# Three more zero fills write 56 KB rows in a decode-attention training kernel on one Trainium2 core

## The chip, the cores and the metric

The kernel runs on one core of one Trainium2 (trn2) chip. The metric is device time in microseconds (us) of one execution. Timed runs of the same kernel agree within about 0.1% here (765.08 to 765.98 us over all timed runs of the kernel before; the execution that was profiled took 766.4 us), so differences below about 1 us in the time need several rounds, and below 0.3 us they can't be seen at all. Engines are named as in the profile: PE multiplies matrices, DVE and ACT work on vectors, POOL issues the zero fills, SP and ACT also issue the other transfers.

Three sources are used. The *page* and the *views* of the profile (groups, waits, timeline, windows) are shown as they stand. The trace behind them also has one record for each DMA packet (here one row of a transfer, or one completion, which is a write of 4 bytes), with queue, start, duration and size; what is read from these is said to come from the packet records, and is of one execution for each kernel.

## The reference, cut to what matters

One decode step of attention with a gated MLP, and the gradients of all inputs. The caches are 32768 positions long, but only the last 4096 positions of each head take part:

```python
B, Sq, D = 2, 1, 512
Hq, Hkv, Sk, Dh = 32, 8, 32768, 128
W = min(4096, max(256, Sk // 4))            # 4096
k = jnp.repeat(k_cache[:, :, Sk - W:, :], rep, axis=1)
v = jnp.repeat(v_cache[:, :, Sk - W:, :], rep, axis=1)
...
_out, _vjp = jax.vjp(_f, A_x, A_k_cache, A_v_cache, A_wq, A_wo, ...)
```

The gradients of the two caches are therefore zero at 28672 of 32768 positions of each of 2 x 16 heads. The output must have these zeros, and writing them is most of what the kernel does: 32 regions of 28672 x 128 bf16 numbers, 7.34 MB each, 235 MB of 327 MB that are moved in all.

## The kernel before: the parts that matter

Zeros come from one tile `zt` in on-chip memory (SBUF) of 128 partitions x 14336 bytes. A fill is a DMA issued from POOL that converts while it copies: the 14336 bytes become 14336 bf16 numbers (28672 B) or, where the output is viewed as 4-byte numbers, 57344 B.

```python
ZR = SK - W                  # 28672 positions
ZG = 112
zt = const.tile([P, ZG * DH], mybir.dt.uint8, name="zt")
...
def zf(o, q, r0, nent, rows, rep=1):         # nent rows of `rows` positions, rep times
    b, hk = divmod(q, HKV)
    nr = nent * rows * rep
    v = o[b, hk, r0:r0 + nr, :]
    w = rows * DH
    if w > ZG * DH:                          # a row of 224 positions: 57344 B
        v = v.bitcast(F32)
        w //= 2
    v = v.rearrange("(r p g) d -> p r (g d)", p=nent, g=rows)
    st = 4 if nent < 16 else 1
    zs = zt[0:nent * st:st, 0:w].unsqueeze(1).to_broadcast([nent, rep, w])
    sw_fill.append(nc.gpsimd.dma_start(out=v, in_=zs))
    return r0 + nr
...
zlong = (0, 1, 3, 5, 7, 11, 12, 16, 17, 18, 19, 22, 23, ...)
zshort = {2: ((5, 8, 2), (120, 68, 3), ...), 4: ..., 20: ...}   # eight fills, divided
...
for qi in range(ZQ - 1):                     # ZQ = 32: 31 fills on POOL's software queue
    r = 0
    whole = (P, ZR // P, 1) if qi in zlong else (P, ZG, ZR // (P * ZG))
    for n, rows, rep in zshort.get(qi, (whole,)):
        r = zf(*zparts[qi], r, n, rows, rep)
```

So an undivided fill in `zlong` is 128 rows of 57344 B; the three that are not (9, 14, 21) are 256 rows of 28672 B. Eight more are cut into pieces, not changed here. The 32nd fill is issued by SP at the very end, in rows of 14336 B.

Beside the fills run four rounds, each of four heads: a 4 MB V load and a 4 MB K load (SP), computation, and two 4 MB stores of gradients (ACT), each load waiting for the store that frees its buffer. Then come the weight gradients and the last fill:

```python
last = nc.sync.dma_start(out=out_6.rearrange("(p k) f -> p k f", k=DK), in_=dw1_st)   # dW1
...
with tc.issue_after(last.ins):
    fin = nc.sync.dma_start(out=v, in_=zs)   # the 32nd fill, after dW1 in SP's order
tc.add_manual_dep(fin.ins, sw_fill[-2].ins.name, ...)   # and after the last but one on POOL
```

Of the kernel before, what the change touches and what calls it, by code (L numbers as in the profile page):

```python
# [16 lines left out]
def kernel(  # L17
# [86 lines left out]
    ZQ = 2 * B * HKV  # L104
    zparts = [(out_2, q) for q in range(B * HKV)] + [(out_3, q) for q in range(B * HKV)]

    zlong = (0, 1, 3, 5, 7, 11, 12, 16, 17, 18, 19, 22, 23, 24, 25, 26, 27, 28, 29, 30)
    zshort = {
        2: ((5, 8, 2), (120, 68, 3), (128, 32, 1), (16, 1, 1)),
        4: ((3, 1, 2), (2, 99, 6), (128, 112, 1), (128, 102, 1), (86, 1, 1)),  # L110
# [564 lines left out]
```

## Time and profile before

| | before |
|---|---|
| time, median (runs) | 765.66 us (3) |
| span of the profiled run | 764.6 us |
| moved | 326.73 MB |
| PE / DVE / ACT busy | 51% / 36% / 28% |
| dW1 store issued (end of computation) | 696.9 us |
| final fill issued, landed | 724.2, 763.4 us |

The page of the kernel before, its parts 1 to 3. The DMA row gives the mean busy share of the 16 DMA engines in 40 equal slices of the span, in tenths; the queue lines give packets, MB, and the share of 16 engines' span:

```profile
span 764.6 us, 9391 instructions
...
PE 388.6 (51%) x4109; PEld 234.4 (31%) x4118; DVE 275.8 (36%) x483; ACT 214.9 (28%) x313; POOL 34.7 (5%) x67
...
DMA  9999999999999999999999999999999999999998
...
DMA packets 12217, 326.73 MB, mean 427 GB/s; under 512 B 2898, under 2 KB 2906, under 8 KB 2934
...
q0 software_dynamic: 7744, 227.55, 70.3%
q1 hardware_dynamic: 2696, 56.63, 20.8%
q10 hardware_dynamic: 1736, 41.95, 13.9%
```

No engine is near its limit except the DMA engines, which never have a free slice. Queue q0 holds the fills of POOL, q1 what SP issues, q10 what ACT issues.

The windows view of the kernel before, three stretches: columns are the stretch, its length, busy time of PE, PEld (PE's weight loads), DVE, ACT and POOL, the clock granted to PE, DMA share, GB/s:

```profile
528.00:556.00 28.00, 16.27 (x272) 12.61 (x270) 13.54 (x26) 10.52 (x10) 1.59 (x3) 0.84 1.03 436
560.00:600.00 40.00, 26.07 (x253) 14.76 (x256) 13.97 (x30) 11.95 (x20) 1.04 (x2) 0.76 1.02 432
725.00:740.00 15.00, 0.00 (x0) 0.00 (x0) 0.00 (x0) 0.00 (x0) 0.00 (x0) 0.50 1.06 434
```

The rate is the same with computation (first two lines) and without (third line): transport doesn't wait for computation. A window counts a packet with the stretch in which it starts, so a short one can read some GB/s too high or too low; counted by overlap, stretches of 20 us from 40 to 760 us carry 429 to 433.

The timeline of SP's DMA issues in the kernel before (start, duration, line of the kernel, what), the last loads and the end:

```profile
479.04 0.54 SPq L210 DMA_DIRECT2D nat<-in_A_v_cache_dram  x1
501.42 0.54 SPq L210 DMA_DIRECT2D nat<-in_A_k_cache_dram  x1
...
696.91 0.33 SPq L639 DMA_DIRECT2D out_dram<-dw  x1
724.24 0.39 SPq L644 DMA_DIRECT2D out_dram<-zt  x1
```

And four lines of its waits views, the last from that of SP's queue (who waited for whom, us in total, times, longest):

```profile
POOL out_dram L101 <- DMA out_dram<-zt: 507.8, 39, 27.3
...
PE tp L387 <- DMA nat<-in_A_v_cache_dram: 126.5, 3, 52.2
...
PE tp L387 <- DMA nat<-in_A_k_cache_dram: 11.3, 2, 9.5
...
SPq L644 <- DMA out_dram<-zt: 26.9, 1, 26.9
```

After the dW1 store at 696.9 us nothing is left but transfers. The final fill then stands behind another fill for 27 us. POOL's issuing is no limit either: it waits 508 us for earlier fills to land.

### The profile page before, as it was taken

Reading aid. Unit: us, or ns where it says so; the run is one execution under the profiler, and the core shown is the slowest. Engines: PE = TensorE matmul, PEld = TensorE weight load, DVE = VectorE, ACT = ScalarE, POOL = GpSimd, SP = SyncE. Lnnn points to the kernel's source line nnn. Section 1 sums busy time; section 2 is a strip of 40 time slices with the busy share of each in tenths; the row PEclk is TensorE's granted clock in tenths of the full one; section 3 lists DMA queues with packets and bytes.
Section 4 is the critical chain, followed back from the end, with each engine's and each line's share of the span. In section 5 each row is a group of like instructions: output and inputs, shape, how many; then the busy total and the mean of one; then the engine's idle time right before and its main releaser. Section 6 shows DMA issues by size and latency. Waiting matters only on the chain.

```text
span 764.6 us, 9391 instructions
## 1 busy us (share of the span) xinstructions
PE 388.6 (51%) x4109; PEld 234.4 (31%) x4118; DVE 275.8 (36%) x483; ACT 214.9 (28%) x313; POOL 34.7 (5%) x67
## 2 busy tenths in 40 slices
PE   0566774477007747830784770038459467594000
PEld 0543553333005534410463320026344333321000
DVE  3234342485003446430554650014344245663000
ACT  0044521455001246530224550002422254153000
POOL 0200100010000000000000000000000000000000
PEclk9986997778556867665596775559859666555555
DMA  9999999999999999999999999999999999999998
GB/s 378 434 410 428 447 420 425 442 438 414 437 423 435 429 435 431 426 433 425 430 430 445 430 422 438 422 436 424 440 442 430 430 425 432 432 427 428 442 409 367
DMA packets 12217, 326.73 MB, mean 427 GB/s; under 512 B 2898, under 2 KB 2906, under 8 KB 2934
## 3 DMA queue, kind: packets, MB, share of 16 engines
q0 software_dynamic: 7744, 227.55, 70.3%
q1 hardware_dynamic: 2696, 56.63, 20.8%
q10 hardware_dynamic: 1736, 41.95, 13.9%
q8 instruction: 32, 0.52, 0.3%
q14 instruction: 9, 0.07, 0.0%
HBM read 45.62 MB, written 280.50 MB: 427 GB/s over the span
## 4 chain that ended last, share of the span: by engine, by line
DMA 32%; PE 31%; DVE 13%; ACT 9%; issue 6%; ACTq 0%; SPq 0%; DVEq 0%
DMA out_dram<-nat 14%; DMA nat<-in_A_v_cache_dram 8%; DMA nat<-in_A_k_cache_dram 7%; PE tp L387 6%; PE ov L421 5%; ACT tring L150 3%; DMA b_bf<-in_B_b_dram 2%; ACT p_bf L455 2%; ACT nat L150 2%; DVE tring L152 2%; PE s_ps L394 2%; DVE nat L152 2%; DVE ds_bf L468 2%; PE wps L588 2%; PE dops L314 2%
## 5 line engine op out<-in xcount | busy, mean ns | idle before, releaser
L387 PE MATMUL tp<-pperm,nat 128*128 128x128 bf16 x1024 | 91.9, 243 | 144.7 <-DMA nat<-in_A_v_cache_dram 126.5
L152 DVE COPY tring<-tp 128x1024 bf16<-128x1024 bf16 (+1 forms) x98 | 65.9, 689 | 179.1 <-PE tp L387 169.4
L387 PEld LDWEIGHTS <-nat 128*128 128x128 bf16 x1024 | 68.5, 109 | 165.1 <-DMA nat<-in_A_v_cache_dram 128.4
L150 ACT CAST nat<-ov 128x512 bf16<-128x512 f32 x160 | 87.7, 589 | 68.8 <-PE ov L421 48.1
L150 ACT COPY tring<-tp 128x1024 bf16<-128x1024 bf16 (+1 forms) x34 | 34.4, 1011 | 228.5 <-PE tp L387 155.1
L152 DVE CAST nat<-ov 128x512 bf16<-128x512 f32 x96 | 65.6, 690 | 59.7 <-PE ov L421 57.1
L101 POOL DMA_DIRECT2D out_dram<-zt x58 | 33.1, 576 | 529.3 <-DMA out_dram<-zt 507.8
L421 PE MATMUL ov<-bd,ds_bf 128*128 128x512 bf16 x124 | 49.4, 472 | 6.6 <-DVE nat L152 3.9
L421 PE MATMUL ov<-bd,p_bf 128*128 128x512 bf16 x123 | 47.3, 451 | 5.5 <-DVE nat L152 1.4
L410 PE MATMUL ps<-t,nat 128*128 128x16 bf16 x1024 | 28.7, 173 | 14.3 <-DVE bd L375 7.2
L410 PEld LDWEIGHTS <-nat 128*128 128x128 bf16 x1024 | 28.7, 103 | 17.1 <-issue 11.9
L394 PEld LDWEIGHTS <-zz 128*32 128x32 bf16 x512 | 17.8, 96 | 33.4 <-issue 23.1
L152 DVE CAST wq<-wps 128x512 bf16<-128x512 f32 x16 | 11.0, 690 | 42.4 <-PE wps L581 42.3
L402 PE MATMUL tp<-ident_bf,p_bf 128*128 128x128 bf16 x64 | 7.6, 312 | 34.9 <-ACT p_bf L455 34.9
L394 PE MATMUL s_ps<-tring,zz 128*32 128x256 bf16 x256 | 19.2, 288 | 11.8 <-ACT tring L150 7.4
L394 PE MATMUL dp_ps<-tring,zz 128*32 128x256 bf16 x256 | 20.5, 326 | 7.1 <-ACT tring L150 4.2
L150 ACT CAST wq<-wps 128x512 bf16<-128x512 f32 x16 | 9.4, 586 | 51.7 <-PE wps L581 51.7
L455 ACT ACTIVATE p_bf<-e_sb,rl 32x512 bf16<-32x512 f32 x16 | 22.8, 1424 | 3.4 <-DVE rl L452 3.2
L468 DVE SCALAR_TENSOR_TENSOR ds_bf<-dp_ps,delta,p_bf 32x512 bf16<-32x512 f32 x16 | 21.7, 1355 | 0.2
L421 PEld LDWEIGHTS <-ds_bf 128*128 128x128 bf16 x128 | 13.1, 110 | 20.6 <-issue 18.3
L421 PEld LDWEIGHTS <-p_bf 128*128 128x128 bf16 x128 | 12.9, 110 | 19.6 <-issue 16.7
L564 PE MATMUL tp<-ident_bf,wq 128*128 128x128 bf16 x128 | 16.8, 248 | 2.3 <-issue 2.3
(195 smaller groups left out, 435.5 us busy)
## 6 DMA issues: line engine op xcount, KB each, us to landing
out_dram<-zt POOLq DMA_DIRECT2D x23, 7168.0 KB, 100.0
out_dram<-nat ACTq DMA_DIRECT2D x8, 4096.0 KB, 40.5
out_dram<-zt POOLq DMA_DIRECT2D x7, 3584.0 KB, 71.3
nat<-in_A_v_cache_dram SPq DMA_DIRECT2D x4, 4096.0 KB, 31.8
nat<-in_A_k_cache_dram SPq DMA_DIRECT2D x4, 4096.0 KB, 26.6
out_dram<-zt SPq DMA_DIRECT2D x1, 7168.0 KB, 39.5
out_dram<-zt POOLq DMA_DIRECT2D x2, 3488.0 KB, 66.9
out_dram<-zt POOLq DMA_DIRECT2D x1, 6120.0 KB, 67.6
```

The source lines that it names most:

```text
L101: sw_fill.append(nc.gpsimd.dma_start(out=v, in_=zs))
L150: nc.scalar.copy(out=out_ap, in_=in_ap)
L152: nc.vector.tensor_copy(out=out_ap, in_=in_ap)
L314: nc.tensor.matmul(dops[0:B, :, :], lhsT=dsT_bf[:, dk, :], rhs=woT[:, :, dk, :], start=(dk == 0), stop=(dk == DK - 1))
L387: nc.tensor.transpose(tp[:, j, :], nat[:, g * CC + half * CH + j, :], pperm[:].rearrange("p b k -> p (b k)"))
L394: nc.tensor.matmul(out_ps[pr * RB:(pr + 1) * RB, half * CH * PB:(half + 1) * CH * PB], lhsT=zbuf[:, pr, o:o + RB], rhs=tT[:, :, pr, :], st ...
L410: nc.tensor.matmul(ps[:], lhsT=nat[:, g * CC + half * CH + cc, :], rhs=cols[half][:, cc, :, g, :], start=(half == 0 and g == 0 and cc == 0 ...
L421: nc.tensor.matmul(ov[:], lhsT=src[:, cc].rearrange("r k b -> r (k b)"), rhs=bd[:, gh * 4:(gh + 1) * 4, :], start=True, stop=True)
L455: nc.scalar.activation(out=p_bf[rb, :, :, pr], in_=e_sb[rb], func=ACT.Copy, scale=rl[rb, 0:1])
L468: nc.vector.scalar_tensor_tensor(out=ds_bf[rb, :, :, pr], in0=dp_c[rb], scalar=delta[rb, 0:1], in1=p_bf[rb, :, :, pr], op0=ALU.subtract, o ...
L564: nc.tensor.transpose(tp[:, jj, :], wq[:, k, n0:n0 + DH], ident_bf[:, :])
L588: nc.tensor.matmul(wps[:], lhsT=o_rows[:, j:N:NJ], rhs=ds_rows[:, :], start=True, stop=True)
```

## The change

The intent is that every undivided fill writes the longer rows: half as many packets for the same bytes.

```diff
-    zlong = (0, 1, 3, 5, 7, 11, 12, 16, 17, 18, 19, 22, 23, 24, 25, 26, 27, 28, 29, 30)
+    zlong = (0, 1, 3, 5, 7, 9, 11, 12, 14, 16, 17, 18, 19, 21, 22, 23, 24, 25, 26, 27, 28, 29, 30)
```

## The prediction

> **What bounds the kernel now.** Transport. The page's DMA row is 9 in 39 of 40 slices; 326.73 MB in 764.6 us are 427 GB/s. In the trace's packet records an engine stands idle for less than 0.1 us (mean of 16) in every 20 us from 20 to 760 us; only the first 5 us and the last 1.9 us are thin (the engines finish between 761.5 and 763.4 us). PE is busy 51%, DVE 36%, ACT 28%. The timeline shows the last computation at about 697 us; after it only transfers run, and the last zero fill (7168 KB, issued by SP at 724.2 us after a wait for another fill) lands at 763.4. So the end is set by bytes over rate. The Trainium skill agrees ("DMA: Bandwidth & Descriptors", Specifications: a fabric ceiling of 435 GB/s); the windows 560:600 and 725:740 show 432 and 434.
>
> **What the change does.** Fills 9, 14 and 21 (7.34 MB each) go from 256 rows of 28672 B to 128 rows of 57344 B. Bytes, DMA count (58 on POOL), dependencies and engines stay; 384 packets leave the software queue (7744 to 7360). In the packet records a 28672 B packet takes 1079 ns median (1082 mean), a 57344 B one 2155 (2150 mean). Two short ones cost 3 to 14 ns more than one long one. 384 pairs over 16 engines: 0.07 to 0.34 us saved. Pool's issue (0.55 us median) hides behind waits for other fills (508 us over 39 waits), so anything saved there is worth nothing.
>
> **What moves.** Packets alternate between queues one by one: at 700:716 us the fills, SP and ACT share 236, 62 and 135 GB/s, the ratio of their rows (57, 14, 33 KB). The skill states that round-robin ("Queues, rings and completion order", Arbitration). So longer fill rows take a larger share from the loads beside them. Fill 9 now runs at about 240 to 267 us beside the second K load, fill 14 at about 357 to 393 beside the third K load, fill 21 at about 490 to 540 beside the last V and K loads. An even split of 32 KB and 28 KB rows gives a load 53%, beside 56 KB rows 36%: 18 us against 27 us for 4 MB. I expect these loads to land 3 to 9 us later, and the computation to end 5 to 15 us later (702 to 712 us). That is off what sets the end: the fills get what the loads lose, a fill of 17 us lies behind the software queue's end, and the engines stay full as long as the last stores are issued before about 740 us.
>
> **Predicted.** 765.3 us, 0.3 below; 8 in 10 between 764.3 and 766.7, mostly for the 1 to 2 us with which the engines finish unequally, which another order of packets can shift. Chances: faster 0.01, same 0.98, slower 0.01.
>
> **What would show it.** Packets in the software queue 7360, no 28672 B packets except in the divided fills; rate beside those fills up by under 1%; the K and V loads named land later; the last computation after 697 us; the final fill still ends about 763 us; DMA row unchanged.
>
> **What would make it wrong.** If the longer rows delay the last stores past 740 us, the tail runs dry and the loss is real. If one DMA engine is slower than the others and gets relief from fewer rows, the end could move by a microsecond or two. If computation has less slack than I read, it would be slower by several us.

## More of the kernel before

A packet record doesn't say on which of the 16 DMA engines it ran.

## The result, and the profile after

| | before | after |
|---|---|---|
| time, median of 6 runs each | 765.51 us | 765.31 us |
| lowest to highest | 765.24 to 765.92 | 765.06 to 765.58 |
| packets in the software queue | 7744 | 7360 |
| second K load complete | 254.4 us | 261.0 us |
| third K load complete | 388.3 us | 397.9 us |
| last V load complete | 507.0 us | 511.7 us |
| last K load complete, 15th and 16th completion | 525.2, 525.8 us | 528.2, 555.6 us |
| dW1 store issued | 696.9 us | 724.6 us |
| last packet of POOL's fills / of all | 745.8 / 763.4 us | 727.2 / 762.1 us |

The ratio is 0.9996, with a 95% interval of 0.9984 to 1.0009: the same. The completions and the last packets come from the packet records: each load posts 16 four-byte completion packets, and the load has landed when the sixteenth has ended.

The page after, the lines that answer to those of before:

```profile
span 763.3 us, 9400 instructions
...
PE 387.6 (51%) x4118; PEld 233.5 (31%) x4118; DVE 275.8 (36%) x483; ACT 214.6 (28%) x313; POOL 34.0 (4%) x67
...
DMA  9999999999999999999999999999999999999998
...
DMA packets 11833, 326.73 MB, mean 428 GB/s; under 512 B 2898, under 2 KB 2906, under 8 KB 2934
...
q0 software_dynamic: 7360, 227.55, 70.5%
```

384 packets fewer, the same bytes, the same rate, the same rows of nines. The windows after:

```profile
528.00:556.00 28.00, 1.52 (x23) 0.85 (x20) 1.04 (x2) 1.01 (x1) 1.06 (x2) 0.58 1.06 434
560.00:600.00 40.00, 20.50 (x331) 15.64 (x330) 17.47 (x29) 12.60 (x13) 0.53 (x1) 0.67 1.02 432
725.00:740.00 15.00, 0.00 (x0) 0.00 (x0) 0.00 (x0) 0.00 (x0) 0.00 (x0) 0.50 1.03 440
```

The first line is the surprise. Between 528 and 556 us PE now works 1.5 us, where it had worked 16.3, while the DMA engines move as much as ever. SP's timeline and the waits after say why and where it goes:

```profile
482.61 0.54 SPq L210 DMA_DIRECT2D nat<-in_A_v_cache_dram  x1
507.46 0.54 SPq L210 DMA_DIRECT2D nat<-in_A_k_cache_dram  x1
...
724.57 0.33 SPq L639 DMA_DIRECT2D out_dram<-dw  x1
725.00 0.42 SPq L644 DMA_DIRECT2D out_dram<-zt  x1
```

```profile
POOL out_dram L101 <- DMA out_dram<-zt: 507.8, 38, 28.4
...
PE tp L387 <- DMA nat<-in_A_v_cache_dram: 130.0, 3, 49.7
...
PE tp L387 <- DMA nat<-in_A_k_cache_dram: 42.8, 4, 25.3
```

PE waits 31.5 us longer for K loads, and one wait, for the last of them, is 25.3 us long. Computation ends 27.7 us later, and none of that reaches the time, which is as before. But the 27 us between the dW1 store and the final fill are used up: the final fill is now issued 0.4 us after that store, so it is SP's order and no longer another fill that holds it.

### The profile page after: what moved, and what is told of

Its sections match the earlier page's. It is cut to its first block, busy times and chain, and to the rows that moved or that the text cites. A ratio compares the mean times of both kernels' runs of the same rounds, so it can differ in the third digit from the quotient of the medians.

```text
span 763.3 us, 9400 instructions
## 1 busy us (share of the span) xinstructions
PE 387.6 (51%) x4118; PEld 233.5 (31%) x4118; DVE 275.8 (36%) x483; ACT 214.6 (28%) x313; POOL 34.0 (4%) x67
## 2 busy tenths in 40 slices
DMA packets 11833, 326.73 MB, mean 428 GB/s; under 512 B 2898, under 2 KB 2906, under 8 KB 2934
## 3 DMA queue, kind: packets, MB, share of 16 engines
q0 software_dynamic: 7360, 227.55, 70.5%
## 4 chain that ended last, share of the span: by engine, by line
DMA 36%; PE 31%; DVE 12%; ACT 9%; issue 6%; ACTq 0%; DVEq 0%; SPq 0%
DMA nat<-in_A_k_cache_dram 18%; DMA out_dram<-nat 15%; PE ov L421 7%; PE tp L387 4%; ACT nat L150 3%; ACT p_bf L455 2%; DMA b_bf<-in_B_b_dram 2%; PE ps L410 2%; DVE nat L152 2%; ACT tring L150 2%; DVE ds_bf L468 2%; PE s_ps L394 2%; PE wps L588 2%; PE dops L314 2%; PE tp L310 1%
## 5 line engine op out<-in xcount | busy, mean ns | idle before, releaser
L421 PEld LDWEIGHTS <-p_bf 128*128 128x128 bf16 x128 | 12.8, 109 | 19.8 <-issue 17.1
L402 PEld LDWEIGHTS <-p_bf 128*128 128x128 bf16 x64 | 6.5, 146 | 36.0 <-ACT p_bf L455 36.0
```

Source lines behind the costliest of these rows:

```text
L402: nc.tensor.transpose(tp[:, cc, :], src[:, half * CH + cc].rearrange("r k b -> r (k b)"), ident_bf[:, :])
L421: nc.tensor.matmul(ov[:], lhsT=src[:, cc].rearrange("r k b -> r (k b)"), rhs=bd[:, gh * 4:(gh + 1) * 4, :], start=True, stop=True)
```

## The experiments

Three questions were open: is it bytes over rate that sets the time; what does a packet cost; and why did computation slip by 27.7 us where 5 to 15 were foreseen? Twelve kernels were run. Those with a single timed run are given without a ratio, and the profiler calls their state unknown; their times lie between 765.45 and 765.80 us, as those of the others.

This table, from the packet records (us), is needed throughout. Each row but the column "time" is from one profiled execution. "Issue" is the issue of the last K load, "15th" and "16th" the ends of its completions, "longest" the longest of its 16 completion packets, "dW1" the issue of the dW1 store.

| run | long rows among 9, 14, 21 | issue | 15th | 16th | longest | dW1 | time |
|---|---|---|---|---|---|---|---|
| before | none | 501.4 | 525.2 | 525.8 | 0.03 | 696.9 | 765.51 |
| after | 9, 14, 21 | 507.5 | 528.2 | 555.6 | 14.83 | 724.6 | 765.31 |
| r_again | 9, 14, 21 | 507.9 | 528.5 | 555.8 | 14.83 | 726.0 | 765.55 |
| only9 | 9 | 502.7 | 526.2 | 527.3 | 0.03 | 695.2 | 765.80 |
| only14 | 14 | 508.0 | 528.2 | 534.4 | 0.03 | 703.6 | 765.45 |
| only21 | 21 | 500.6 | 524.6 | 524.9 | 0.03 | 699.2 | 765.88 |
| not21 | 9, 14 | 509.5 | 536.1 | 543.8 | 7.43 | 716.0 | 765.28 |
| not9 | 14, 21 | 507.9 | 528.7 | 556.0 | 14.83 | 726.5 | 765.49 |
| quarter21 | 9, 14; 21 with 14 KB rows | 507.7 | 528.4 | 528.5 | 0.03 | 699.0 | 765.52 |
| all_short | none, nor any other | 481.6 | 508.0 | 508.3 | 0.03 | 660.9 | 766.04 |
| all_quarter | all with 14 KB rows | 477.7 | 499.9 | 500.0 | 0.03 | 652.7 | 766.92 |

### 1. The changed kernel once more

Edit: none.

> The changed kernel again, unaltered, for a second profile. Theory A (the late completion of the last K load on one DMA engine belongs to the kernel): the same straggler shows again, 15 completions near 528 us and one over 545 us, with a completion packet of over 12 us, and the last computation ends at 718 to 731 us. Rival B (chance of one execution): the last K load completes on all 16 engines within 5 us and the computation ends at 702 to 712 us. Both: 764.3 to 766.3 us in time.

Measured: 15 completions by 528.5 us, one at 555.8 with a packet of 14.83 us, dW1 at 726.0 us, 765.55 us. Theory A holds: the late completion belongs to the kernel and isn't one execution's chance.

### 2. Fill 21 alone, and fills 9 and 14 without it

```diff
-    zlong = (..., 7, 9, 11, 12, 14, 16, ..., 19, 21, 22, ...)
+    zlong = (..., 7, 11, 12, 16, ..., 19, 21, 22, ...)        # only21
+    zlong = (..., 7, 9, 11, 12, 14, 16, ..., 19, 22, ...)     # not21
```

> Only fill 21 has long rows; 9 and 14 are short again. Theory: the lateness comes from the rows that stand beside the last K load, so the last K load still completes over 15 us after its 15th engine and the last computation ends at 715 us or later. Rival: each of the three fills adds about a third of the 27.7 us, so the end of computation is at 703 to 709 us. Time in both cases 765 to 766 us, software queue 7616 packets.

> Fills 9 and 14 long, 21 short. Theory: the last K load lands within 5 us on all engines, computation ends at 699 to 706 us (only the 3 to 6 us with which the earlier loads were late). Rival (a third per fill): 712 to 718 us. Time 765 to 766 us in both cases.

Measured: with fill 21 alone the last K load was not late at all (524.9 us) and dW1 was issued at 699.2 us. That refutes both the theory and the rival, which had it at 703 to 709. With 9 and 14 alone dW1 came at 716.0 us, within what the rival had named, but a third per fill can't be: fill 21 alone adds 2.3 us. Times: 765.88 us (ratio 1.0003, 0.9988 to 1.0018) and 765.28 us (0.9998, 0.9984 to 1.0012).

The packet records show the misreading. In the kernel before, the 28672 B packets at 490 to 510 us belong to the divided fill 20, which has a piece of 112-position rows too; its last large piece (the only one with rows of 28160 B) ends at 529.0 us. Fill 21's own rows start at about 522 us, when the last K load is all but landed (525.8). So in the kernel before, and in only21, fill 21 hardly meets a load. In the changed kernel that piece of fill 20 is done at 524.5 us, 4.5 us earlier, and the K load is issued 6.0 us later: now they meet. The new theory was that 9 or 14 shifts the load, and 21 then punishes it.

### 3. One fill at a time, and the pair that matters

```diff
+    zlong = (..., 7, 9, 11, 12, 16, ..., 19, 22, ...)         # only9
+    zlong = (..., 7, 11, 12, 14, 16, ..., 19, 22, ...)        # only14
+    zlong = (..., 7, 11, 12, 14, 16, ..., 19, 21, 22, ...)    # not9
```

> Only fill 9 long. Theory: fill 9 makes the second V and K loads complete late (about 238 and 261 us instead of 232 and 254), and the fills behind gain, but fill 14 stays short: the third V load completes at 366 to 371 us, the third K load at 388 to 393. The last K load is issued 2 to 5 us later than before, and the computation ends at 699 to 708 us. If fill 9 alone makes most of the shift: the last K load completes at over 535 us and computation ends at 712 us or later.

> Only fill 14 long. The second V and K loads are as in the kernel before (231.9 and 254.4 us). Theory: the third K load completes 5 to 9 us later (393 to 397 us), the last K load is issued 2 to 5 us later, computation ends at 699 to 708 us. If fill 14 alone makes most of the shift: the last K load completes at over 535 us and computation ends at 712 us or later.

> Fills 14 and 21 long, 9 short. Theory (fill 14 delays the issue of the last K load by 6 to 7 us, and only then do fill 21's rows stand beside its last rows on the slowest engine): the last K load is issued at 506 to 509 us, 15 engines complete near 528 us and one at 545 us or later, with a completion packet of over 8 us; computation ends at 715 us or later. Rival (fill 9 is needed too): all complete by 536 us and computation ends at 698 to 707 us. Time 765 to 766 us in both cases.

Measured: fill 9 alone makes the second V and K loads late, at 238.5 and 262.1 us, as expected, but that is absorbed before the end: the last K load is issued only 1.3 us later than before, less than the 2 to 5 expected, and dW1 comes at 695.2 us, 1.7 us *earlier* than before (699 to 708 expected, a miss). Fill 14 alone makes the third K load land at 396.9 us, within the 393 to 397 expected, and the last K load is issued 6.6 us later, more than the 2 to 5; dW1 at 703.6 us, within the 699 to 708 expected. With 14 and 21 together, named in advance as the pair that is enough, the whole picture is back: issue at 507.9, fifteen completions by 528.7, the sixteenth at 556.0 with a packet of 14.83 us, dW1 at 726.5 us. The waits view of that run (fills 14 and 21):

```profile
PE tp L387 <- DMA nat<-in_A_k_cache_dram: 41.1, 4, 23.1
```

The longest wait, 23.1 us, answers to the 25.3 us of the changed kernel. Fill 9's change is not needed for the slip of the last load.

### 4. The size of fill 21's rows

In addition to fills 9 and 14 with long rows:

```diff
-            whole = (P, ZR // P, 1) if qi in zlong else (P, ZG, ZR // (P * ZG))
+            whole = (P, ZR // P, 1) if qi in zlong else (P, ZG // 2, 2 * ZR // (P * ZG))
```

> Fills 9 and 14 long, fill 21 as 512 rows of 14336 B. Theory after the first runs: 9 and 14 shift the last K load so that fill 21 stands beside its last rows on the slowest engine, and there the load and its completion wait for a count of fill rows, so the row size sets the lateness: with 57344 B the load completed at 555.6 us, with 28672 B at 543.8, so with 14336 B at 535 to 540 us; the longest completion packet, 14.8 and 7.4 us before, is at most 4.5 us; computation ends at 706 to 713 us. Rival (waits are for a number of bytes, and what the two runs showed came of another shift): completion and end of computation as with 28672 B, 543 to 545 and 715 to 717 us.

Measured: the last K load landed at 528.5 us on all sixteen, still earlier than the 535 to 540 expected, and dW1 came at 699.0 us (706 to 713 expected). With everything else alike and the load issued at the same time within 2 us, the sixteenth completion came at 555.6 us beside rows of 57344 B, at 543.8 beside 28672 B and at 528.5 beside 14336 B. The direction is what the theory says, the size was off on the low side. The 28672 B case also varies: with two fills removed far later (experiment 6) the same rows gave 533.7 us, with no long completion packet, and dW1 at 703.5 instead of 716.0. The long rows show no such spread: 555.6, 555.8, 556.0 and 555.7 us in four executions (after, r_again, not9, and the changed kernel with two fills removed). For 14336 B there is one execution, so its spread isn't known.

How the lateness comes about can be said in part. Of the 27.4 us between the fifteenth and the sixteenth completion, the last data packet of the load ends at 538.7 us in the packet records, and the completion packet runs from 540.8 to 555.6. Its 14.83 us are 6.9 times a long row's 2.155 us; the 7.43 us in not21 are 6.9 times a short row's 1.079.

The data part follows from turn-taking. In the changed kernel five rows of fill 21 start at 511.4, 513.5, 516.9, 520.3 and 523.8 us, and all others from 525.4 us on. From 515.6 us a load packet of 32768 B begins where such a row ends, a step of 3.4 us, and the load's late packets (529.5, 532.9, 536.2 us) continue that step: it fits one DMA engine that reached fill 21 some 14 us before the others and carries its eight load packets between long rows. Where fill 21 has other rows and one engine is ahead, the step is 2.3 us for 28672 B (only14, not21_drop2) and 1.75 us for 14336 B (quarter21), and the load's data end at 533.3, 532.6 and 528.4 us instead of 538.7. The engine is inferred from ends and starts that meet, as the records don't name it.

The completion's part is less regular. The Trainium skill ("DMA: Bandwidth & Descriptors", section "Queues, rings and completion order", HWDGE ordering) says that the completion write lands only after every earlier write from that engine, across its queues; a packet that spans seven fill rows fits that.

The wait isn't peculiar to this load. In the kernel before, all sixteen completions of the first V load, beside fill rows of mostly 57344 B, have packets of 8.5 to 10.6 us (four or five rows); with no long rows at all (all_short of experiment 5) they have 0.03 us. In every kernel with fill 9 long, the second V load's sixteenth completion has 10.6 or 12.7 us and comes at 238.4 to 238.9 us instead of the 231.2 to 232.0 of the kernel before, only14, only21, not9 and before_drop2. But a short row is no guarantee: in all_quarter, with rows of 14336 B, one completion of the first V load took 10.35 us and one of the third K load 7.67. Why one engine is ahead, and how many rows a completion has to wait for, stays open. That a single late completion is no new thing is shown by the kernel before: its third V load had fifteen completions by 361.5 us and the sixteenth at 365.7.

### 5. What a packet costs

```diff
-    zlong = (0, 1, 3, 5, 7, 9, 11, ...)
+    zlong = ()                                  # all_short: 28672 B; all_quarter: also the edit of 4
```

> All 23 undivided fills of the software queue as 256 rows of 28672 B: 10304 packets, 2560 pairs more than before. If a pair costs 6 to 14 ns more than one long packet, over 16 engines: 1.0 to 2.2 us slower than before, 766.5 to 767.7 us. Rival (the size of rows is worth nothing at all, the 0.2 us were noise): within 0.3 us of before. The loads get more than with long rows, so computation ends at 690 us or earlier, and the time does not follow that.

> All 23 undivided fills as 512 rows of 14336 B: 16192 packets. A fixed cost of 3 to 7 ns for each packet gives 5888 more packets than all short rows, over 16 engines 1.1 to 2.6 us more than all short rows, so 767 to 770 us. Rival (no cost for a packet): 765.5 us. Loads get most of the engines beside such rows (70% by even turns), so computation ends earlier still, under 685 us, without gain.

Measured over five runs each: 766.04 us (ratio 1.0009, 0.9997 to 1.0022) and 766.92 us (ratio 1.0022, 1.0008 to 1.0036), both below the ranges expected, and all_short above its rival's 0.3 us too. Against the kernel before, all_quarter has 8448 packets more (16192 instead of 7744) and takes 0.0022 x 765.4 = 1.7 us longer: 1.7 us x 16 engines / 8448 = 3.2 ns for a packet, and the interval excludes zero (0.0008 to 0.0036 are 1.2 to 5.2 ns). For all_short the same sum gives 0.7 us x 16 / 2560 = 4.3 ns, with an interval that includes zero. Of the two figures that the prediction had for a pair, 3 ns from medians and 14 from means, the first came close, but partly by luck, as the duration of a packet is no measure of its cost: in all_quarter the median packet of 14336 B takes 552 ns, so that two take 25 ns more than one of 28672 B, while the times of all_quarter and all_short differ by 1.0 us or 2.7 ns for a packet. The packets of an engine overlap in the records (DMA shares above 1.00 in the windows).

In these two kernels the loads get more of the engines, and dW1 is issued at 660.9 and 652.7 us, 36 and 44 us earlier than before, with a time that is a little longer. The page of all_quarter shows the queue at work:

```profile
DMA  9999999999999999999999999999999999999998
...
q0 software_dynamic: 16192, 227.55, 71.7%
```

So computation may end anywhere between 653 and 727 us, and the time moves only with the packets.

### 6. Where the slip would cost

If transport sets the time, taking bytes away must shorten it in proportion; and where it has become short enough, the end of computation must show. Fills 28 and 29 are written when all loads are done, so they were left out. The result is wrong: two regions stay unwritten, and only out_3, which holds them, fails.

```diff
         for qi in range(ZQ - 1):
+            if qi in (28, 29):
+                continue
             r = 0
```

> The kernel before without fills 28 and 29, 14.68 MB that are written after the last loads (the result is wrong on purpose: these two regions stay unwritten). Transport theory: bytes over 431 GB/s, 34.1 us less, so 730.5 to 732.5 us, computation ends at about 690 to 698 us and the final fill still follows without a gap. Rival (the chain of computation and stores sets the end): less than 10 us are gained.

> The changed kernel without fills 28 and 29 (wrong on purpose in the same way). If its computation still ends at about 718 to 725 us, what must follow it is the dW1 store and the final fill, 1.83 and 7.34 MB or 21 us at 431 GB/s, so the engines run dry and the time is 740 to 748 us: 9 to 16 us more than the same cut gives in the kernel before. Rival (the lateness of computation is harmless even here, or doesn't recur): 730 to 732 us, as the other.

> Fills 9 and 14 long, 21 short, without fills 28 and 29 (wrong on purpose). Theory: in the shortened kernel the end is the end of computation plus the final fill and the completion, 25.7 us as in the changed kernel without the two fills (computation 725.0, time 750.7). With computation ending at 716 to 717 us the time is 741 to 743 us. Rival (the 19 us that the changed kernel lost there come of something other than the end of computation): 750 us or 731 us.

| kernel without fills 28 and 29 | dW1 store issued | time (4 runs) | ratio to the full kernel before |
|---|---|---|---|
| as before | 695.9 us | 731.50 us | 0.9557 (0.9544 to 0.9570) |
| with 9, 14, 21 long | 724.6 us | 750.66 us | 0.9801 (0.9788 to 0.9815) |
| with 9, 14 long | 703.5 us | 731.54 us | 0.9557 (0.9541 to 0.9573) |

The cut of 14.68 MB gave the kernel before 34 us, as bytes over 431 GB/s has it (730.5 to 732.5 us expected, 731.50 measured). It gave the changed kernel 15 us; by the 2% rule that ratio is called unclear, its interval lies at 0.9788 to 0.9815. 0.9801 / 0.9557 = 1.026: in the shortened kernel the same change is a loss of 2.6%. The loss was expected, its size wasn't: 740 to 748 us were expected, 750.66 measured (748.34 to 751.17), as 26 us and not 21 lie between the dW1 store's issue and the end. The windows of the changed kernel without the two fills, and below them those of the kernel before without them, show where:

```profile
600.00:690.00 90.00, 63.19 (x607) 33.74 (x606) 44.17 (x74) 32.56 (x57) 0.50 (x1) 0.71 1.14 429
694.00:708.00 14.00, 12.27 (x33) 5.02 (x34) 9.09 (x18) 5.86 (x10) 0.00 (x0) 0.50 0.00 1
```

```profile
600.00:690.00 90.00, 64.46 (x428) 30.26 (x429) 49.14 (x75) 34.37 (x60) 0.00 (x0) 0.58 1.21 431
694.00:708.00 14.00, 1.36 (x4) 0.28 (x2) 1.10 (x3) 1.17 (x2) 0.00 (x0) 0.50 0.98 420
```

From 694 to 708 us the changed kernel moves 1 GB/s: its DMA engines have nothing left while PE still works 12.3 us of 14. The other moves 420 GB/s in that stretch. The third kernel, not21_drop2, missed its expected 741 to 743 us: its computation ended at 703.5 us and not at 716, so transport still set its time. The rule in the expectation survives (end of computation plus about 26 us, if that is later than what the bytes allow: 703.5 + 26 is below 731.5), but this run didn't test it, since its premise failed. What it adds is a limit: the prediction's 740 us for the last stores, less the 34 us of the cut, is 706 us. A dW1 store at 703.5 us cost nothing, one at 724.6 us cost 19.2 us.

## Why the prediction was right

- **What bounds the kernel: right.** Bytes over rate. Experiment 6 shows it directly: 14.68 MB less, 34 us less. Experiment 5 shows the other side: computation ending 36 to 44 us earlier gains nothing. What holds the rate at 431 GB/s no run varied, so its nearness to the ceiling that the prediction cites doesn't show that this ceiling binds.
- **The gain: too small to see, so its sum wasn't tested by this change.** Predicted 0.3 us, from 0.07 to 0.34; measured -0.2 by the medians, with an interval of about -1.2 to +0.7 us. By the 3.2 ns that all_quarter shows, 384 packets over 16 engines are worth 0.08 us, at the low end of the sum. The change is invisible in the time by its own size; that the medians agree with the 0.3 us foretold to a tenth is luck.
- **Longer rows take a larger share, so loads land later: right for fills 9 and 14, in part by a way not named.** The second K load, issued as before, landed 6.6 us later. Of the third K load's 9.6 us, 6.9 are its later issue: it waits for a gradient store, and from that store's issue to the K load's it took 38.9 us instead of 34.5. The prediction named only loads. The last V load's 4.7 us lie in the 3 to 9 foretold by luck: fill 21 wasn't beside it, and 3.6 of them are its later issue. One execution can move a landing too: the kernel before had its third K load complete at 388.3 us, and at 394.2, for one completion of sixteen, without fills 28 and 29, which come far later.
- **"Fill 21 now runs at about 490 to 540 beside the last V and K loads": wrong.** Rows of the same size belong to the divided fill 20. Fill 21 begins when the last K load has nearly landed, and changing it alone moves that load by less than 1 us (only21).
- **"I expect ... the computation to end 5 to 15 us later": mis-sized.** It ended 27.7 us later. The missing term is the last K load: not 3 to 9 us but 29.8 us late, as one of its sixteen completions came 27.4 us after the fifteenth. Fills 14 and 21 make this together (not9), neither alone does (only14, only21). The prediction counted shares of the rate for all engines alike, and had no term for one engine that is ahead, nor for a completion that waits.
- **"Off what sets the end": right, with less room than it looked.** The limit named, last stores issued before about 740 us, held with 724.6. By that limit some 43 us were in hand before and about 15 after, and experiment 6 shows what happens when they are used up.
- **The final fill ends at about 763 us: right** (762.1 us). The engines finish between 759.9 and 762.1 us instead of 760.4 and 763.4; the profiled spans differ by 1.3 us with that, one execution each, and that of the kernel before was a long one (766.4 us); the medians differ only by 0.2.

None of the versions with all their output clearly beats both, and the runs say why: at 431 GB/s, 326.73 MB take 758 us, and what is left, the start, the uneven finish and the launch, is 1% of the time.

## What to carry to other kernels

When the transfer engines are full from start to end, ask of a change only whether it changes bytes, the cost of a byte, or the time at which the engines run dry; how late the computation becomes doesn't matter until then, and a trial with fewer bytes shows how far away it is. The length of a row on one queue acts like a priority: it decides how much the other queues get, and can lengthen the wait for their last completion, even where it does nothing for the rate. A load is complete when its slowest part is, so look at each of its completions, not at the average rate. Before saying which transfer stands beside which, identify it by something that only it has; a row size shared by two fills misled this prediction.

## What the Trainium skill lacked or had wrong

- "DMA: Bandwidth & Descriptors", "Queues, rings and completion order", Arbitration, states the turn-taking but not its consequence: shares follow row sizes. Here 236, 62 and 135 GB/s at 700 to 716 us for rows of 57344, 14336 and 32768 B.
- The same page states that completions wait for earlier writes across queues, but no size for it. Here single completions took 14.83 us beside rows of 57344 B, 7.43 us beside 28672 B (not21), and up to 10.35 us beside 14336 B (all_quarter).
- "Perfetto Trace Analysis", "What 'DMA-bound' means", says that large descriptors are what matter when DMA engines are the limit, and the section gives no size at which this ends. At these sizes they hardly do: 14336 B in place of 28672 and 57344 B cost 1.7 us of 765 (0.2%), 3.2 ns for a packet.
- "HBM Reference", Specifications (TRN2), gives about 425 GB/s for a core that streams alone. Stretches of 20 us from 40 to 760 us in the kernel before carry 429 to 433 GB/s, mostly writes; whether other cores of the chip were idle isn't on record.
- No page gives a size for how far the last of a load's sixteen completions can trail the fifteenth when another queue is busy: 4.2 us in the kernel before (third V load), 27.4 us after (last K load).
